# Pairs of tiles of one expert as seven block products for eight: a mixture-of-experts stage on one Trainium2 core

## The chip, the cores and the metric

The kernel runs on 1 core of one Trainium2 chip. The metric is the device time of one execution in microseconds (us). All runs below were in the fast state, but for one of the six of e1_static_after, and for single runs whose state is unknown; both are said where they come. Ratios are the mean time of one kernel's fast runs over the mean time of the other kernel's fast runs of the same rounds, on the same chip; so they are not quite the ratio of the medians that are quoted beside them.

Two sections of a run are used throughout, both read from the timeline of TensorE. The *stretch* goes from the first of the 48 small products with which the routing places its tokens (shortly before the tiles of the second round begin) to the end of the last product. The *tail* goes from there to the end of the span. What lies before the stretch, mostly attention, is the same code in every kernel here, yet it ended anywhere from 226 to 236 us after the start, in both kernels and in every experiment. That alone moves single times by 8 us or so; stretch and tail are free of most of it. The granted clock has a part in it: before the stretch, the profile of before (stretch from 234.71 us) has 0.50 for 10.24 us from 102.7 and for 3.41 us from 212.0, and that of after (226.49) has 1.00 from 9.2 us on.

## The reference

```python
def reference(q, k, v, w_gate, w_local, w1, w2):      # shortened
    x = attention(q, k, v)                            # (8, 576, 512), half local heads, half strided
    logits = x @ w_gate                               # 8 experts
    for b, s in every token in order:
        fresh = argmax(logits[b, s])
        e = fresh if s == 0 or sigmoid(x[b, s] @ w_local) < 0.5 else prev_e
        prev_e = e
        h = np.maximum(x[b, s] @ w1[e], 0.0)          # w1[e]: 512 x 1024
        out[b, s] = softmax(logits[b, s])[e] * (h @ w2[e])   # w2[e]: 1024 x 512
```

All is fp32. Which expert a token has depends on the data, so the kernel sorts the 4608 tokens on the chip into tiles of 128 tokens of one expert. For these inputs there are 6 early tiles (routed while attention still runs), then 30 whole tiles and 2 mixed ones (two half tiles of two experts).

## The kernel before

One tile is 32 hidden products into two PSUM banks, 4 transposes of the next tile, 8 output products, and one scatter by GpSimd. VectorE copies the transposed tile and works out the gates of its tokens, no more.

```python
    def hidden(self, j):
        nc = self.nc
        w1, xT, hT = self.w1t[j], self.xT[j], self.hT[j]
        for g in range(FK // self.HB):
            ps = self.bank()
            for i in range(self.HB):
                c = slice((g * self.HB + i) * P, (g * self.HB + i + 1) * P)
                for kk in range(DK):
                    ins = nc.tensor.matmul(ps[:, i], lhsT=w1[:, kk, c], rhs=xT[:, kk * P:(kk + 1) * P],
                                           start=(kk == 0), stop=(kk == DK - 1))
            nc.scalar.activation(hT[:, g * self.HB:(g + 1) * self.HB], ps, Act.Relu)
        return ins.ins

    def output(self, j):                              # cut: the branch for mixed tiles
            for kk in range(FK):
                ins = nc.tensor.matmul(ps, lhsT=self.hT[j][:, kk], rhs=self.w2t[j][:, kk, :],
                                       start=(kk == 0), stop=(kk == FK - 1))
        nc.scalar.activation(y, ps, Act.Copy, scale=self.pt[j])
        nc.gpsimd.indirect_dma_start(out=self.out, in_=y, ...)

    def run(self, ctx, second, check):                # cut to the loop
        for j, t in enumerate(self.T):
            ahead = self.weights(j + 2) if j + 2 < NT else []
            ...                                       # gathers, three tiles ahead
            if t["rd"] is self.r2 and NT_MIN - NE <= t["i"] < self.r2.whole:
                ...                                   # used: the number of whole tiles, read from SBUF
                ctx.enter_context(tc.If(used > t["i"]))
            ins = (self.hidden_mixed if "halves" in t else self.hidden)(j)
            ...                                       # first half of the weight loads
            if j + 1 < NT:
                self.turn_x(j + 1)
            ins = self.output(j)
            ...                                       # second half of the weight loads
```

Tiles that may or may not exist stand under nested conditions, so one jump at the end skips those that do not.

Of the kernel before, what the change touches and what calls it, by code (L numbers as in the profile page):

```python
# [18 lines left out]
P = 128  # L19
# [33 lines left out]
NT = NT_MAX + NM  # L53

MIXED = (14, 25)
SKIP = 8192
# [4 lines left out]
AHEAD = 3  # L61

# [39 lines left out]
class Round:  # L102
# [3 lines left out]
    def __init__(self, pool, whole, nm=0):  # L106
        self.whole, self.n = whole, whole + nm
        self.gi = pool.tile([P, self.n], I32, name="gi")
        self.si = pool.tile([P, self.n], I32, name="si")
        self.oh = pool.tile([P, self.n, E], F32, name="oh")  # L110
        self.et = pool.tile([1, self.n + 1 + 2 * nm], I32, name="et")
# [74 lines left out]
def passes(tc, careful, q, k, vl, vs, wg, w1, w2, out, xd, c, sums, bad):  # L186
    with ExitStack() as ctx:
        keep = ctx.enter_context(tc.tile_pool(name="keep", bufs=1))
        r1 = ctx.enter_context(tc.tile_pool(name="slots1", bufs=1))
        r1 = Round(r1, NE)  # L190
        r2 = ctx.enter_context(tc.tile_pool(name="slots2", bufs=1))
        r2 = Round(r2, NT_MAX - NE, NM)
# [18 lines left out]
        with ExitStack() as part:  # L211
            psr = part.enter_context(tc.tile_pool(name="psr", bufs=2, space=PSUM))
            rp = part.enter_context(tc.tile_pool(name="rp2", bufs=1))
            ex.run(part, route(tc, rp, psr, B, c, codes, r2, early),
                   None if careful else lambda: bounds(tc, rp, psr, sums, bad))
# [284 lines left out]
def route(tc, rp, pp, nb, c, codes, rd, early):  # L500
# [4 lines left out]
    R, CN, n, whole = nb * E, LT * nb, rd.n, rd.whole  # L505
# [61 lines left out]
    nc.tensor.matmul(ps[0:R, 0:1], lhsT=c.less[0:E, 0:R], rhs=nt[0:E], start=True, stop=True)  # L567
    first = nn[:, 3:4]
    if final:
        nc.vector.tensor_copy(first, ps[0:R, 0:1])  # L570
        tiles, skipped = nt, nn[:, 2:3]
    else:
        nc.vector.tensor_scalar(first, ps[0:R, 0:1], float(NE), None, Alu.min)
        tiles, skipped = nn[:, 2:3], None
        nc.vector.tensor_scalar(tiles, first, -1.0, float(NE), Alu.mult, Alu.add)
        nc.vector.tensor_tensor(tiles, tiles, nt, op=Alu.min)
        nc.vector.tensor_copy(early, tiles[0:E])
    end = rp.tile([E, 1], F32, name="end")
    nc.vector.tensor_tensor(end, first[0:E], tiles[0:E], op=Alu.add)
    over = rp.tile([E, whole], F32, name="over")  # L580
    nc.vector.tensor_scalar(over, c.io[0:E, 0:whole], end, None, Alu.is_ge)
    thr, base = nn[:, 4:5], nn[:, 5:6]
    nc.vector.tensor_scalar(thr, nn[:, 2:3], float(P), nn[:, 1:2], Alu.mult, Alu.subtract)
    if final:
        nc.vector.tensor_tensor(base, first, skipped, op=Alu.subtract)
        nc.vector.tensor_scalar(base, base, float(P), nn[:, 1:2], Alu.mult, Alu.add)
    else:
        nc.vector.tensor_scalar(base, first, float(P), nn[:, 1:2], Alu.mult, Alu.add)
# [4 lines left out]
    if final:  # L593

        last, far = nn[:, 9:10], nn[:, 10:11]
        nc.vector.scalar_tensor_tensor(last, nt, float(P), thr, Alu.mult, Alu.add)
        nc.vector.tensor_tensor(far, first, nt, op=Alu.add)
        nc.vector.tensor_scalar(far, far, -float(P), float(P * whole), Alu.mult, Alu.add)
        nc.vector.scalar_tensor_tensor(far, rank, float(HT), far, Alu.mult, Alu.add)
        more = rp.tile([R, S], F32, name="more")  # L600
        nc.vector.tensor_scalar(more, cum, last, far, Alu.is_gt, Alu.mult)
        nc.vector.tensor_tensor(slot, slot, more, op=Alu.add)
# [5 lines left out]
    nc.tensor.matmul(ps[:, 0:whole], lhsT=c.ones, rhs=over, start=True, stop=True)  # L608
    if final:
        nc.tensor.matmul(ps[0:1, n:n + 1], lhsT=c.ones[:, 0:1], rhs=nt[0:E], start=True, stop=True)  # L610
        nc.tensor.matmul(ps[0:1, n + 1:n + 1 + NH], lhsT=c.er[0:E], rhs=whose, start=True, stop=True)
        for h in range(2):
            nc.tensor.matmul(ps[:, whole:n], lhsT=c.half[h], rhs=whose.rearrange("e (m h) -> e h m", h=2)[:, h],
                             start=(h == 0), stop=(h == 1))
# [4 lines left out]
    nc.vector.tensor_scalar(rd.et[:, 0:n], ps[0:1, 0:n], float(E - 1), None, Alu.min)  # L619
    if final:  # L620
        nc.vector.tensor_copy(rd.et[:, n:], ps[0:1, n:n + 1 + NH])
    nc.vector.tensor_tensor(rd.oh, across(c.io[:, 0:E], [P, n, E]), spread(ps[:, 0:n], [P, n, E]), op=Alu.is_equal)
# [43 lines left out]
class Ring:  # L666


    def __init__(self, pool, n, shape, name):
        self.tiles = [pool.tile(shape, F32, name=f"{name}{i}") for i in range(n)]  # L670

    def __getitem__(self, j):
        return self.tiles[j % len(self.tiles)]


class Experts:

# [4 lines left out]
    def __init__(self, ctx, tc, xd, w1, w2, out, c, r1, r2):  # L682
        self.tc, self.nc = tc, tc.nc
        self.xd, self.w1, self.w2, self.out, self.c = xd, w1, w2, out, c
        self.r2 = r2
        xp = ctx.enter_context(tc.tile_pool(name="xp", bufs=1))
        self.w1t = Ring(xp, 2, [P, DK, F], "w1t")
        self.w2t = Ring(xp, 2, [P, FK, D], "w2t")
# [4 lines left out]
        self.pe = Ring(xp, 2, [P, E], "pe")  # L693
        self.pt = Ring(xp, 2, [P, 1], "pt")
        self.T = [dict(rd=r1, i=i, rows=BE * S) for i in range(NE)] + [dict(rd=r2, i=i, rows=N) for i in range(r2.whole)]
        for m, j in enumerate(MIXED):
            self.T.insert(j, dict(rd=r2, i=r2.whole + m, rows=N, halves=[r2.n + 1 + 2 * m + h for h in range(2)]))
        self.used = 0

    def weights(self, j, h=0):  # L700

        nc, t = self.nc, self.T[j]
        w1 = lambda e: self.w1[bass.ds(e, 1)].rearrange("o (k p) f -> p (o k) f", p=P)
        w2 = lambda e: self.w2[bass.ds(e, 1)].rearrange("o (k p) f -> p (o k) f", p=P)

        at = t["halves"][h] if "halves" in t else t["i"]

        def load(dst, src, part):
            if ("e", h) not in t:
                t["e", h] = nc.values_load(t["rd"].et[0:1, at:at + 1], engines=[ET.SP], min_val=0, max_val=E - 1,  # L710
# [3 lines left out]
            nc.sync.dma_start(out=dst[:, s], in_=src(t["e", h])[:, s])  # L714

        to = ((self.w1x, w1), (self.w2x, w2)) if h else ((self.w1t[j], w1), (self.w2t[j], w2))
        return [lambda a=a, part=part: load(*a, part) for a in to for part in range(2)]

    def gather(self, j):
        t = self.T[j]  # L720
        self.nc.gpsimd.indirect_dma_start(  # L721
            out=self.xg[j], out_offset=None, in_=self.xd[0:t["rows"]],
            in_offset=bass.IndirectOffsetOnAxis(ap=t["rd"].gi[:, t["i"]:t["i"] + 1], axis=0))

    def turn_x(self, j):
        nc, t = self.nc, self.T[j]
        x, ps = self.xg[j], self.psx[j]
        for kk in range(DK):
            nc.tensor.transpose(ps[:, kk * P:(kk + 1) * P], x[:, kk * P:(kk + 1) * P], self.c.ident)  # L729
        ins = nc.vector.tensor_copy(self.xT[j], ps)  # L730

        with self.tc.issue_after(ins.ins):
            nc.vector.tensor_tensor(self.pe[j], x[:, D:DX], t["rd"].oh[:, t["i"]], op=Alu.mult)
            nc.vector.tensor_reduce(self.pt[j], self.pe[j], axis=AX.X, op=Alu.add)

    def bank(self):
        self.used += 1
        return self.psh[self.used - 1]

    def hidden_mixed(self, j):  # L740

        nc, xT = self.nc, self.xT[j]
        for f in range(2):
            ps = self.bank().rearrange("p a b -> p (a b)")
            for kk in range(DK):
                for h, w1 in enumerate((self.w1t[j], self.w1x)):
# [5 lines left out]
    def turn_h(self, j, f):  # L752
        nc, ps = self.nc, self.bank()
        for i in range(self.HB):
            k = f * self.HB + i
            ins = nc.tensor.transpose(ps[:, i], self.h[:, k * P:(k + 1) * P], self.c.ident)
# [129 lines left out]
```

## Time and profile before

| | before |
|---|---|
| time, median of 3 runs | 746.26 us (744.17 to 748.84) |
| profiled run: span, stretch, tail | 750.2, 496.05, 19.44 us |
| TensorE, VectorE, ScalarE busy | 96%, 25%, 20% |
| weights and other hardware-queue traffic | 216.87 MB, 81.7% of 16 DMA engines |
| one tile, start to start | 14.45 us |

The stretch is 66% of the span and it is TensorE alone: the prediction below shows the lines and how they are read. Two more lines are needed later, the gathers and scatters of GpSimd (instructions, busy us, mean ns of one, and idle time before them):

```profile
L721 POOL DMA_INDIRECT xg<-xd,gi x41 | 40.3, 983 | 381.2 <-issue 139.0
L788 POOL DMA_INDIRECT out_dram<-y,si x38 | 40.8, 1075 | 266.5 <-ACT y L787 253.0
```

and the end of it, the last scatter of the timeline (start, length, and what it waited for), which starts 1.0 us after the last product ended at 730.7 us:

```profile
731.77 0.98 POOL L788 DMA_INDIRECT out_dram<-y,si  x1 [13.45 <-ACTq L211]
```

### The profile page before, as it was taken

How to read it: one execution, taken by the hardware profiler on the slowest of the kernel's cores; microseconds unless marked ns; L12 is line 12 of the kernel's file. 1: busy time of each engine (PE TensorE's matmuls, PEld its weight loads, DVE VectorE, ACT ScalarE, POOL GpSimd, SP SyncE). 2: the span in 40 equal slices, each digit the busy share in tenths (PEclk: the TensorE clock that was granted, in tenths of full speed). 3: DMA queues.
4: the chain of work that ended last, by engine and by line, in shares of the span. 5: the costliest groups of instructions: out<-in, count | busy, mean ns of one | idle time of the engine just before them, and what ended most of it. 6: DMA issues, size and time to landing. Idle time of an engine off the chain costs nothing. (4 is left out here: it accounts for less than half of the span.)

```text
span 750.2 us, 12762 instructions
## 1 busy us (share of the span) xinstructions
PE 722.9 (96%) x5132; PEld 546.1 (73%) x5132; DVE 183.8 (25%) x614; ACT 148.3 (20%) x267; POOL 84.4 (11%) x100
## 2 busy tenths in 40 slices
PE   7999999999999999999999999999999999999990
PEld 6999898977777667767736776776657677677660
DVE  5777877755360000000010000000010000000000
ACT  2555434541111111111111111111111111111110
POOL 1000002001012111111111111111111111111100
PEclk9999979999999999999999999999999999999995
DMA  9988778986868999999998989999997998999993
GB/s 345 346 275 272 266 216 306 337 305 213 305 236 287 328 335 324 348 403 395 376 352 287 324 310 345 372 401 398 368 319 284 345 330 307 334 335 314 323 321 118
DMA packets 95655, 238.24 MB, mean 318 GB/s; under 512 B 10526, under 2 KB 19742, under 8 KB 95584
## 3 DMA queue, kind: packets, MB, share of 16 engines
q1 hardware_dynamic: 88736, 216.87, 81.7%
q0 software_dynamic: 6320, 20.36, 7.0%
q8 instruction: 44, 0.72, 0.4%
q14 instruction: 27, 0.22, 0.1%
q10 hardware_dynamic: 528, 0.07, 0.1%
HBM read 218.26 MB, written 19.55 MB: 317 GB/s over the span
## 5 line engine op out<-in xcount | busy, mean ns | idle before, releaser
L768 PEld LDWEIGHTS hps<-xgT,w1t 128*128 128x128 f32 x2304 | 262.4, 192 | 16.0 <-issue 15.5
L768 PE MATMUL hps<-xgT,w1t 128*128 128x128 f32 x2304 | 263.8, 275 | 0.3 <-DVE xgT L730 0.3
L785 PE MATMUL yps<-w2t,hT 128*128 128x512 f32 x576 | 254.9, 596 | 0.0
L785 PEld LDWEIGHTS yps<-w2t,hT 128*128 128x128 f32 x576 | 107.2, 191 | 121.6 <-issue 121.6
L730 DVE COPY xgT<-tps 128x512 f32<-128x512 f32 x39 | 27.0, 691 | 424.8 <-PE tps L729 424.7
L770 ACT ACTIVATE hT<-hps 128x512 f32<-128x512 f32 x72 | 43.0, 597 | 216.3 <-PE hps L768 208.7
L721 POOL DMA_INDIRECT xg<-xd,gi x41 | 40.3, 983 | 381.2 <-issue 139.0
L787 ACT ACTIVATE y<-yps,pt 128x512 f32<-128x512 f32 x38 | 26.1, 687 | 261.2 <-PE yps L785 245.4
L788 POOL DMA_INDIRECT out_dram<-y,si x38 | 40.8, 1075 | 266.5 <-ACT y L787 253.0
L333 PE MATMUL sps<-qt,kt 64*128 64x96 f32 (+2 forms) x704 | 50.6, 290 | 5.3 <-DMA kt<-in_k_dram 5.0
L333 PEld LDWEIGHTS sps<-qt,kt 64*128 64x128 f32 (+2 forms) x704 | 44.5, 197 | 10.0 <-issue 8.2
L337 ACT ACTIVATE e<-sps 128x576 f32<-128x576 f32 (+1 forms) x64 | 39.9, 651 | 19.3 <-PE sps L333 18.2
L380 PE MATMUL vps<-vlt,e 128*96 128x96 f32 x384 | 40.8, 264 | 0.2 <-PE sps L333 0.2
L380 PEld LDWEIGHTS vps<-vlt,e 128*96 128x96 f32 x384 | 37.3, 176 | 4.1 <-issue 3.1
L380 PE MATMUL vps<-vst,e 108*108 108x108 f32 (+1 forms) x320 | 38.2, 275 | 1.0 <-DVE xs L391 0.8
L380 PEld LDWEIGHTS vps<-vst,e 108*108 108x108 f32 (+1 forms) x320 | 34.8, 185 | 2.7 <-PE vps L380 0.9
L340 DVE TENSOR_TENSOR e<-e,maskL 128x576 f32<-128x576 f32 x32 | 23.2, 754 | 17.9 <-ACT e L337 17.7
L340 DVE TENSOR_TENSOR e<-e,maskS 108x648 f32<-108x648 f32 (+1 forms) x32 | 23.1, 753 | 9.5 <-ACT e L337 9.5
L423 ACT COPY xT<-xps 128x324 f32<-128x324 f32 (+1 forms) x32 | 18.7, 684 | 33.0 <-PE xps L417 31.9
L729 PE MATMUL tps<-ident,xg 128*128 128x128 f32 x156 | 23.8, 274 | 0.0
L729 PEld LDWEIGHTS tps<-ident,xg 128*128 128x128 f32 x156 | 18.3, 142 | 0.2
L391 DVE TENSOR_TENSOR xl<-vps,rc 96x384 f32<-96x384 f32 x32 | 17.3, 545 | 0.5
(177 smaller groups left out, 318.8 us busy)
## 6 DMA issues: line engine op xcount, KB each, us to landing
w1t<-in_w_dram SPq DMA_DIRECT2D x80, 1024.0 KB
w2t<-in_w_dram SPq DMA_DIRECT2D x80, 1024.0 KB
kt<-in_k_dram SPq DMA_DIRECT2D x15, 608.0 KB
qt<-in_q_dram SPq DMA_DIRECT2D x15, 576.0 KB
vlt<-in_vl_dram SPq DMA_DIRECT2D x8, 780.0 KB
vst<-in_vs_dram SPq DMA_DIRECT2D x8, 650.0 KB
xd<-xl SPq DMA_DIRECT2D x8, 576.0 KB
w1x<-in_w_dram SPq DMA_DIRECT2D x4, 1024.0 KB
```

The costliest lines, as they stand in the source:

```text
L333: st["pe"] = nc.tensor.matmul(ps[0:kb, h, i * w:(i + 1) * w], lhsT=kt[r, u.i2, c:c + kb], rhs=qt[r, u.i2, c:c + w], start=True, stop=True)
L337: nc.scalar.activation(ev, ps[0:kb, :, 0:m * w], Act.Exp, bias=0.0, scale=1.0 / DH ** 0.5)
L340: nc.vector.tensor_tensor(blocks(ev, m), blocks(ev, m), mask, op=Alu.mult)
L380: nc.tensor.matmul(ps[0:w, o:o + w], lhsT=u.e[0:kb, h, i * w:(i + 1) * w], rhs=vt[0:kb, u.i2, u.t0 + i, c:c + w], start=True, stop=True)
L721: self.nc.gpsimd.indirect_dma_start(out=self.xg[j], out_offset=None, in_=self.xd[0:t["rows"]], in_offset=bass.IndirectOffsetOnAxis(ap=t["r ...
L729: nc.tensor.transpose(ps[:, kk * P:(kk + 1) * P], x[:, kk * P:(kk + 1) * P], self.c.ident)
L730: ins = nc.vector.tensor_copy(self.xT[j], ps)
L768: ins = nc.tensor.matmul(ps[:, i], lhsT=w1[:, kk, c], rhs=xT[:, kk * P:(kk + 1) * P], start=(kk == 0), stop=(kk == DK - 1))
L770: nc.scalar.activation(hT[:, g * self.HB:(g + 1) * self.HB], ps, Act.Relu)
L785: ins = nc.tensor.matmul(ps, lhsT=self.hT[j][:, kk], rhs=self.w2t[j][:, kk, :], start=(kk == 0), stop=(kk == FK - 1))
L787: nc.scalar.activation(y, ps, Act.Copy, scale=self.pt[j])
L788: nc.gpsimd.indirect_dma_start(out=self.out, in_=y, in_offset=None, bounds_check=N - 1, oob_is_err=False, out_offset=bass.IndirectOffsetOn ...
```

## The change

Two whole tiles of one expert become a pair. Its 256 tokens by 512 inputs, and the weights, are each cut into 2 x 2 blocks, and each layer is done as seven block products for eight (Strassen's form in Winograd's arrangement). The block sums of the weights, of x and of h go to VectorE; four of the seven products of a layer are added up in one PSUM bank, and ScalarE copies the bank out between them. An odd tile of an expert stays single. The pairs 0 to 8 and the two mixed tiles, which always exist, come first; then eight places for singles under nested conditions; then places for seven more pairs under nested conditions. With these inputs 4 singles and 4 of those pairs exist: 13 pairs in all.

```diff
+    def sums_b(self, t, blocks):
+        v, (b11, b12, b21, b22) = self.nc.vector, blocks
+        v.tensor_tensor(t[:, 0], b12, b11, op=Alu.subtract)
+        v.tensor_tensor(b12, b22, b12, op=Alu.subtract)
+        v.tensor_tensor(t[:, 1], b22, t[:, 0], op=Alu.subtract)
+        v.tensor_tensor(t[:, 2], b21, t[:, 1], op=Alu.subtract)
...
+    def hidden_pair(self, j):                       # cut: names of the blocks, product and row
+        self.sums_b(self.t2, self.blocks_w(w2))
+        product(chain, a11, b11, True)
+        nc.scalar.copy(out=p, in_=chain)
+        product(b7, s3, t3, True)
+        product(chain, s2, t2, False)
+        nc.scalar.copy(out=u, in_=chain)
+        product(b2, a12, b21, True)
+        row(b2, p, flat[0])
+        nc.vector.tensor_tensor(u, b7, u, op=Alu.add)
+        product(chain, s1, t1, False)
+        nc.scalar.copy(out=v, in_=chain)
+        row(b7, v, flat[3])
+        product(b4, a22, t4, True)
+        row(b4, u, flat[2])
+        product(chain, s4, b22, False)
+        nc.scalar.activation(flat[1], chain, Act.Relu)
+        self.sums_a(self.hs, hs)
...
+    def output_pair(self, j):                       # the same form, 256 columns, and two scatters
...
+        singles, pairs = count(1, E), count(0, PAIR_MAX)
+        with ExitStack() as chain:
+            for j in range(first, last):
+                chain.enter_context(tc.If(singles > j - first))
+                run(j)
+        for j in range(last, len(U)):
+            ctx.enter_context(tc.If(pairs > U[j]["pair"]))
+            run(j)
```

Here `product` is one block product (8 calls of matmul in the hidden layer, 4 in the output layer), and `row` adds a bank to a saved part on VectorE and applies the ReLU on ScalarE. In the order of a unit, the x sums and the first-layer weight sums of the next unit follow the hidden products of this one, before its output products. The rest of the diff (new slots in the routing, PSUM banks as one ring of eight, buffers) is cut.

## The prediction

> **What bounds the kernel now.** I read the page's busy shares and slices first, then the groups, then the instructions in order of time late in the run, then what TensorE waited for.
>
> ```profile
> PE 722.9 (96%) x5132; PEld 546.1 (73%) x5132; DVE 183.8 (25%) x614; ACT 148.3 (20%) x267; POOL 84.4 (11%) x100
> ...
> DVE  5777877755360000000010000000010000000000
> ...
> DMA  9988778986868999999998989999997998999993
> ...
> L768 PE MATMUL hps<-xgT,w1t 128*128 128x128 f32 x2304 | 263.8, 275 | 0.3 <-DVE xgT L730 0.3
> ...
> L785 PE MATMUL yps<-w2t,hT 128*128 128x512 f32 x576 | 254.9, 596 | 0.0
> ```
>
> TensorE is busy 96% of the span; DVE is all but idle after slice 12, which is where the expert stage begins; the DMA engines are nearly full there. Busy TensorE is not yet a bound, since weights that just arrive would look alike. The idle columns decide: 0.3 us before all 2304 hidden products and 0.0 before all 576 output products. Nothing makes TensorE wait, so only less work on it helps. The timeline gives the unit cost:
>
> ```profile
> 687.25 7.31 PE L768 MATMUL hps<-xgT,w1t 128*128 128x128 f32 x64
> 694.40 0.60 PE L729 MATMUL tps<-ident,xg 128*128 128x128 f32 x4
> 694.83 7.03 PE L785 MATMUL yps<-w2t,hT 128*128 128x512 f32 x16
> 701.70 7.31 PE L768 MATMUL hps<-xgT,w1t 128*128 128x128 f32 x64
> ```
>
> From start to start: 7.15 us for 64 hidden instructions (111.7 ns each), 0.43 us for 4 transposes, 6.87 us for 16 output instructions (429.3 ns each); 14.45 us a tile. The source has 32 hidden and 8 output products per tile, so an fp32 product is two instructions. The groups' means (275 and 596 ns) [...] are not what one costs; the spacing is.
>
> **How many pairs.** Counting the tokens per expert from the inputs gives 6 early tiles, then 30 whole and 2 mixed ones, which the trace confirms (72 evictions of hT, two per whole tile; 38 of y). Per expert the 30 are 4, 3, 4, 3, 3, 4, 4, 5: 13 pairs and 4 singles. Not all 36 whole tiles gain, only 26.
>
> [...] At N=256, which this kernel lacks in this stage, [...] the line through the two measured spacings gives 217.6, which I use. [...]
>
> ```profile
> L340 DVE TENSOR_TENSOR e<-e,maskL 128x576 f32<-128x576 f32 x32 | 23.2, 754 | 17.9 <-ACT e L337 17.7
> ```
>
> [...] The trace has two long ones on TensorE's sequencer:
>
> ```profile
> L211 PEldq COMPARE_BRANCH  x6: 65/76/6040, 667.0 to 731.0; - x6
> ...
> L130 PEldq COMPARE_BRANCH  x1: 6806/6806/6806, 731.6 to 731.6; - x1
> ```
>
> The skipped tiles cost 6.04 us of branch, but from about 724.2, some 6.5 us before the last product ended: the sequencer runs ahead, and it is hidden. [...]
>
> **The change, part by part.**
> Hidden products of a pair: seven block products of 8 calls, 56 calls or 112 instructions, at the same 128 columns: 112 x 111.7 = 12.51 us, where two tiles take 14.30. Saved 1.79.
> Output products: seven of 4 calls, 28 calls or 56 instructions, at 256 columns: 56 x 217.6 = 12.19 us against 13.74. Saved 1.55; the fixed cost per instruction eats some of the eighth, since 56 short instructions replace 32 long ones.
> Transposes: 8, 0.86 us, unchanged. A pair is thus 25.56 us for 28.90, 3.34 less, and 13 pairs save 43.4 us.
>
> Added on DVE[...]: eight block sums of the two weights over 1024 elements, 8 x 1.22 = 9.8; four sums each of h (512) and x (256), 2.8 + 1.7; four PSUM additions of 512 and four of 256, about 2.7 + 1.6; gates 0.3. That is 18.9 us in 25.6, 74%: it fits, with DVE's total rising to about 400 us. ACT: about 7.9 us a pair, 31%. Both lie beside the products as long as order allows.
>
> Order matters, so I laid one steady pair out from the built order of instructions, time zero at its first hidden product (1.79 us each). DVE runs the next pair's first weight sum (after the fifth product frees its buffer, 9.0 to 10.2), the row for h22, the in-place weight sum, the row for h21 (11.9 to 12.5), another weight sum (to 13.6), then three sums of h; the one that the third output product needs is ready at about 15.6. That product starts at 12.51 + 0.86 + 2 x 1.74 = 16.85. Margin 1.2 us: no stall in steady state. The interleaved bank gives every chain copy (0.69 us) a whole product to hide behind.
>
> Moved: weights are fetched once per pair. About 31 sets of 4 MB instead of 42, so the DMA share should fall from nine tenths to about seven. That saves no time now, as TensorE never waited for DMA; it protects the result.
>
> What I charge:
> First pair: its gathers begin one tile earlier than needed; one follows a scatter (0.7 us ACT, 1 us POOL, 1 us its own issue, 6.5 us to landing, about 9) where the transposes ask at 7.6. About 1 us.
> Mixed tiles: their hT copies stand behind weight sums in DVE's queue, about 1.2 us each, 2.4 in all.
> Leaving the singles: these are nested conditions with code behind them now. TensorE drains, loads the pair count, branches; in the old kernel's tail that took 0.9 us (load at 731.2, branch at 731.6, last product over at 730.7). I charge 1.1. But the SP's way out waits for all its DMA lanes, and unneeded prefetches (two singles that do not exist) land about 8.3 us after the last product, as the old tail shows. So the second dynamic pair's w1 is asked for at about +9.5 us and lands at +14 and +17; DVE's sum of it stands ahead of rows that the current pair needs; the h sum comes at about 21.8 instead of 18.0. Charge 3.8.
> Route: 42 columns for 35 in one string of 48 small products, 0.3. Short waits, 0.2 a pair, 2.6. A second scatter at the end, 0.5.
> Sum of charges 1 + 2.4 + 1.1 + 3.8 + 0.3 + 2.6 + 0.5 = 11.7. So 746.3 - 43.4 + 11.7 = 714.6; I say 714 us.
>
> **Rivals.**
> First, DVE becomes the bound. At 74% it has no room for a wrong order; if each DVE row costs 0.2 us more [...] (some 32 rows a pair) the margin of 1.2 is gone and each pair waits 2 or 3 us: 13 x 2.5 = 33, about 745 us, no gain. Against it: [...] back to back they overlap a little (the 0.69 us copy at 709.49 is followed by the next DVE instruction at 710.09). For it: TensorE now has waits on DVE and ACT inside every pair where it had none[...].
> Second, the branch structure costs more: [...] 6 us that the sequencer cannot hide, because semaphores inside a pair hold it back, at the pair conditions or leaving the singles. One such 6 us gives 720; five, on every dynamic pair, 740. Against: fall-through branches are 65 to 76 ns, and only the exits jump.
> Third, weights were the hidden bound and fewer bytes help too. Against: 0.0 us of waiting; then nothing comes beyond the 43.4, and the best case is about 703 us.
> Fourth, the 256-column products are slower than the line says, say 235 ns: 56 x 17 ns is 1 us a pair, 13 us, 727.
>
> **Range and chances.** The product arithmetic is firm: it rests on spacings that repeat to the hundredth, so 703 is a floor. The charges are soft, mostly upward. Range 707 to 724. Two per cent faster is below 731.3: it would take charges of 28 us, more than twice mine, so 0.94 faster, 0.05 same, 0.01 slower.
>
> **What would show it.** Right: pair products spaced 111.7 and about 217 ns; a steady pair 25.6 us from start to start; TensorE idle before its products under 15 us in all, most of it once, in the first pair after the singles, with DVE or a w1 load as what ended it; TensorE busy about 680 us; DVE about 400; DMA near seven tenths; the tail after the last product still about 19 us (730.7 to 750.2). Wrong: idle before the third output product in every pair means that the DVE margin was mis-sized; a pair of 27 us or more without idle means the 256-column spacing was; a gap with nothing running on any engine at the singles' exit means the branch.

## The result, and the profile after

| | before | after |
|---|---|---|
| time, median of 4 runs each, same rounds | 745.21 us (743.17 to 748.84) | 719.61 us (716.16 to 724.57) |
| ratio of the fast runs, 95% interval | | 0.9656 [0.9586, 0.9726] |
| profiled run: span | 750.2 us | 714.5 us |
| stretch, tail | 496.05, 19.44 us | 464.24, 23.77 us |
| start of the stretch | 234.71 us | 226.49 us |

The profiled runs differ by 35.7 us, but 8.2 of that lies before the stretch, in code that did not change: the profile of before had one of the slow attention stages and that of after a quick one. The change itself is worth 31.8 us in the stretch and costs 4.3 in the tail, 27.5 in all, in keeping with the 25.6 between the medians.

The page of the changed kernel, parts 1, 2 and 3 (busy time; tenths in 40 slices; one DMA queue):

```profile
PE 673.8 (94%) x5244; PEld 577.7 (81%) x5244; DVE 399.6 (56%) x894; ACT 192.0 (27%) x360; POOL 100.7 (14%) x103
...
PE   7999999999999999999999999999999979999960
...
DVE  6777888755273348656366664558610026676630
...
DMA  9988779985878996785867857786678989755660
...
q1 hardware_dynamic: 71136, 170.73, 67.9%
```

TensorE has 49 us less to do, VectorE 216 us more, and the traffic fell by 46 MB: all three are close to what was foreseen (TensorE about 680 us busy, VectorE about 400, the traffic down from nine tenths). TensorE's row is full but for the first slice, the 33rd, and the end. VectorE's row shows where the singles are, by two zeros. A steady pair in the timeline, from the start of its first product to the start of the next pair's (start, length, and the number of instructions last):

```profile
285.66 1.95 PE L839 MATMUL bank<-xT,w1t 128*128 128x128 f32 x16
287.44 1.95 PE L839 MATMUL bank<-xs,w1t 128*128 128x128 f32 x16
...
298.16 1.04 PE L839 MATMUL bank<-ident,xg 128*128 128x128 f32 x8
299.03 1.89 PE L839 MATMUL bank<-w2t,h 128*128 128x256 f32 x8
300.76 1.89 PE L839 MATMUL bank<-t,h 128*128 128x256 f32 x8
302.49 1.89 PE L839 MATMUL bank<-t,hs 128*128 128x256 f32 x8
...
311.12 1.95 PE L839 MATMUL bank<-xT,w1t 128*128 128x128 f32 x16
```

The reader is to take starts, not lengths: 1.79 us a hidden product (16 instructions, 111.7 ns each), 0.87 for the transposes, 1.727 an output product (8 instructions, 215.9 ns each, for the 217.6 that were interpolated), and 25.46 us for the pair. Nothing waits in it. The tightest place is the sum of h that the third output product needs; of another pair, the sum on VectorE and the product:

```profile
393.49 0.68 DVE L813 TENSOR_TENSOR hs<-hs,h 128x512 f32<-128x512 f32 x1
...
395.20 1.03 PE L839 MATMUL bank<-t,hs 128*128 128x256 f32 x4
```

The sum is done at 394.17, 1.03 us before the product starts (1.2 had been worked out from the order of the built instructions); the count of 4 is only where the view was cut off. The waits of TensorE in the stretch, from the list of waits (total us, times, longest):

```profile
PE bank L839 <- issue: 5.2, 1, 5.2
...
PE bank L839 <- DMA xg<-xd,gi: 1.7, 2, 1.2
PE bank L839 <- DVE hs L813: 1.3, 2, 0.9
...
PE bank L970 <- DVE hT L944: 0.3, 1, 0.3
```

One entry of 5.2 us, once, with nothing named as its cause, stands out. It lies where the singles end and the next pair begins. The timeline there, cut to four instructions:

```profile
573.62 7.03 PE L974 MATMUL bank<-w2t,hT 128*128 128x512 f32 x16
585.83 3.55 PE L839 MATMUL bank<-xT,w1x 128*128 128x128 f32 x16 [5.17 <-issue]
589.17 2.09 PE L839 MATMUL bank<-xs,w1x 128*128 128x128 f32 x16
591.01 0.18 DVE L805 TENSOR_TENSOR pe<-xg,oh 128x16 f32<-128x16 f32 x1 [11.68 <-DMA xg<-xd,gi]
```

and the branches of the conditions on TensorE's sequencer in that window (shortest, median and longest in ns; the two starts):

```profile
L1074 PEldq COMPARE_BRANCH  x2: 4256/5235/6214, 574.1 to 580.8; - x2
```

The last product of the last single ends about 580.6. The first branch, 6.2 us from 574.1, runs while the products still go: it is hidden, as before the change (6.04 us from 724.2, with the last product over at 730.7). The second begins at 580.8, when TensorE is empty, and takes 4.3 us in the open. Then the first product of the pair takes 3.34 us from start to start instead of 1.79 and the second 1.93: the record of the granted clock has 1.00 in the gap and until 586.05, 0.2 us after the first product began, and 0.50 for 3.41 us from there. VectorE, meanwhile, has stood 11.7 us before the gate of the pair after, whose gathers GpSimd issued only when it had left the singles; its sums come late, and the third output product of this pair waits 0.93 us more.

What the whole passage costs can be read from the transposes: the ones of a single that does not exist begin at 573.19, those of the second pair after the singles at 600.03, those of the third at 626.67 (the first pair's were done before the singles). Without a loss the steps would be 0.43 + 6.87 + 12.51 = 19.81 us and 25.47; they are 26.84 and 26.64. The loss is 7.0 + 1.2 = 8.2 us. The expectations quoted below say 8.6, because they measure against the run without conditions and count the 0.43 us of those useless transposes too.

At the end, two scatters where there was one:

```profile
688.64 1.02 POOL L980 DMA_INDIRECT out_dram<-y,si  x1 [17.61 <-DVE y L907]
693.51 1.01 POOL L980 DMA_INDIRECT out_dram<-y,si  x1 [3.85 <-DVEq L132]
```

and GpSimd's way out of the pair conditions (semaphore waits, the longest 5546 ns; then INC_SWDGE_SEM, which took 1.81 us and is called the closing of GpSimd's DMA queue here):

```profile
L218 POOLq EVENT_SEMAPHORE  x4: 17/43/5546, 693.7 to 699.5; - x4
...
L218 POOLq INC_SWDGE_SEM  x1: 1814/1814/1814, 699.6 to 699.6; - x1
```

The first scatter landed at 692.67; the second began at 693.51, 4.9 us after the first. (The wait is put down to a DVE sequencer instruction here; in e9, where the same two scatters stand earlier, it is put down to the landing of the first, 3.88 us.) GpSimd's long semaphore wait, at the end of the conditions, runs from 693.79 to 699.34; the second scatter landed at 699.30. Before the change it closed the same queue at 731.8, straight after the one scatter at 731.77, which landed at 740.83. The tail is 23.77 us, of which the prediction knew 19.9.

### The profile page after: what moved, and what is told of

The parts are those of the page before. It is cut to its first block, busy times and chain, and to the rows that moved or that the text cites. A ratio compares the mean times of both kernels' runs of the same rounds, so it can differ in the third digit from the quotient of the medians.

```text
span 714.5 us, 13302 instructions
## 1 busy us (share of the span) xinstructions
PE 673.8 (94%) x5244; PEld 577.7 (81%) x5244; DVE 399.6 (56%) x894; ACT 192.0 (27%) x360; POOL 100.7 (14%) x103
## 5 line engine op out<-in xcount | busy, mean ns | idle before, releaser
L783 POOL DMA_INDIRECT xg<-xd,gi x44 | 48.0, 1091 | 250.9 <-DVE rc L394 112.9
L956 PEld LDWEIGHTS bank<-xgT,w1t 128*128 128x128 f32 x640 | 72.6, 192 | 3.1 <-issue 1.9
L956 PE MATMUL bank<-xgT,w1t 128*128 128x128 f32 x640 | 73.6, 276 | 0.9 <-DVE xgT L801 0.9
L974 PE MATMUL bank<-w2t,hT 128*128 128x512 f32 x160 | 70.3, 592 | 0.0
L839 PE MATMUL bank<-xs,t 128*128 128x128 f32 x416 | 50.7, 275 | 0.0
L839 PE MATMUL bank<-t,hs 128*128 128x256 f32 x208 | 49.4, 380 | 1.3 <-DVE hs L813 1.3
L839 PEld LDWEIGHTS bank<-xs,t 128*128 128x128 f32 x416 | 48.5, 192 | 0.0
L839 PEld LDWEIGHTS bank<-xT,w1t 128*128 128x128 f32 x384 | 45.7, 192 | 2.6 <-issue 2.1
L839 PE MATMUL bank<-xT,w1t 128*128 128x128 f32 x384 | 47.4, 276 | 0.0
L839 PE MATMUL bank<-xs,w1t 128*128 128x128 f32 x384 | 46.8, 275 | 0.0
L839 PE MATMUL bank<-w2t,h 128*128 128x256 f32 x192 | 45.4, 379 | 0.0
```

What stands on the lines that cost most here:

```text
L783: self.nc.gpsimd.indirect_dma_start(out=u["xg"][:, a] if "pair" in u else u["xg"], out_offset=None, in_=self.xd[0:u["rows"]], in_offset=ba ...
L839: self.end = fn(*args, **kw).ins
L956: ins = nc.tensor.matmul(ps[:, i * P:(i + 1) * P], lhsT=w1[:, kk, c], rhs=xT[:, kk * P:(kk + 1) * P], start=(kk == 0), stop=(kk == DK - 1))
L974: ins = nc.tensor.matmul(ps, lhsT=hT[:, kk], rhs=w2[:, kk, :], start=(kk == 0), stop=(kk == FK - 1))
```

## The experiments

The theory after reading the two traces: (a) the pair arithmetic is right, and VectorE has a margin of 1 us that nothing steady uses up; (b) what was lost is lost at the conditions, 8 us where the singles end and 4 in the tail. The rivals: VectorE is the bound and paces the pairs; or the short waits in every pair, or the first pair, hold the loss; and for the way out, that it is the branch alone, the gathers alone, or the weights. Losses at the way out are computed as in the section above, from transposes to transposes, for each kernel against its own products and the period of its own pairs after the singles. The table collects what follows, all from the profiled runs:

| run | time, median us | ratio to before | stretch | tail | steady pair | loss at the way out |
|---|---|---|---|---|---|---|
| before | 743.8 to 747.4 | 1 | 496.05 | 19.44 | 28.90 (two tiles) | |
| after | 719.61 | 0.9656 | 464.24 | 23.77 | 25.47 | 8.2 |
| r0_after | 724.68 | 0.9687 | 466.69 | 23.92 | 25.47 | 8.8 |
| e1_static_after | 704.66 | 0.9427 | 454.78 | 14.93 | 25.47 | 0 |
| e2_static_before | 743.54 | 0.9973 | 495.61 | 13.48 | | |
| e3_five_slots | 721.52 | 0.9678 | 464.54 | 23.71 | 25.47 | 8.5 |
| e4_eight | 761.72 | 1.0203 | 501.45 | 24.74 | 28.98 | 1.5 |
| e5_output_seven | 742.12 | 0.9908 | 480.43 | 24.36 | 27.25 | 1.3 |
| e6_hidden_seven | 755.71 | 1.0083 | 494.01 | 24.33 | 27.85 | 10.5 |
| e7_dve_one | 732.36 | one run | 470.40 | 24.12 | 25.60 | 7.9 |
| e8_dve_four | 753.36 | one run | 492.22 | 24.14 | 25.95; 28.41 and more under conditions | 11.5 |
| e9_pairs_first | 710.46 | 0.9530 | 459.32 | 19.45 | 25.47 | 3.3 |
| e10_five_early | 713.47 | 0.9569 | 457.49 | 23.83 | 25.47 | 1.3 |
| e11_eight_early | 720.89 | 0.9690 | 465.04 | 24.51 | 25.47 | 8.5 |

All of them gave the right result. The 95% intervals of the ratios are 0.004 to 0.007 to each side; they are given where they matter.

### r0_after: the changed kernel again, in five rounds

No edit.

> The changed kernel once more, to have its ratio with more rounds and a second profile. Expected ratio 0.965 within 0.006. If the traces' difference is the whole story, the stretch from the start of the 48 route products to the last product is 464 us again (496 in the kernel before) and the tail after the last product 24 us (19.5 before). The attention stage differs by some 8 us between the two profiles at hand although its code is the same: that should vary from run to run in both kernels.

Measured: 724.68 us median (717.32 to 726.00, 6 runs), ratio 0.9687 [0.9633, 0.9740]. The 5.5 us gap at the same place is there again, so it belongs to the kernel and not to one run. The stretch is 2.4 us longer than in the first profile, and most of that is the first pair: TensorE waited 1.95 us for a gather (0.53 and 1.18 in two parts in the first profile), and the 16 output products that followed took 8.57 us from start to start for 6.87, a loss of 1.70 us. By the author's estimate that is a lower clock: 3.41 us at a granted 0.50, as the first profile has them after its gap, would cost as much.

### e1_static_after and e2_static_before: no conditions at all

Both kernels with the counts of these inputs written in, which gives the right result for these inputs only.

```diff
 # e1_static_after: E singles -> 4, PAIR_MAX pairs -> 13, and
-        with ExitStack() as chain:
-            for j in range(first, last):
-                chain.enter_context(tc.If(singles > j - first))
-                run(j)
-        for j in range(last, len(U)):
-            ctx.enter_context(tc.If(pairs > U[j]["pair"]))
-            run(j)
+        for j in range(first, len(U)):
+            run(j)
 # e2_static_before: r2.whole tiles -> 30, and
-                ctx.enter_context(tc.If(used > t["i"]))
```

> The changed kernel with the counts of this data written in (4 singles, 13 pairs) and no conditions. Main theory (leaving the singles costs 5.2 us of branch, about 1.7 us of cold TensorE clock and 1 us of late DVE sums, and the conditions lengthen the tail): the stretch falls by about 8 us to 456, the tail from 24 to 19 or less, in all 10 to 14 us under the changed kernel, about 707 us. Rival (the conditions are hidden, and the pairs themselves are what is slower than worked out): within 3 us of the changed kernel.

> The kernel before with its 30 tiles written in and no conditions on tiles. Main theory: its conditions are hidden (TensorE never waits), so the stretch stays 496 us and only the tail can shorten, by 0 to 3 us: same within 0.5%. If it gains as much as the static pair kernel does, conditions cost both kernels alike and are no reason for the shortfall.

Measured: 704.66 us (698.36 to 708.29, the 5 fast runs; a sixth of 709.67 counts as slow and is left out), ratio 0.9427 [0.9368, 0.9486], and 743.54 us (736.89 to 746.29, 6 runs), ratio 0.9973 [0.9922, 1.0023]. Without conditions the changed kernel is 20 us quicker, 9.5 to 11.9 of it in the stretch and 8.9 in the tail. The kernel before has the same stretch as with conditions (495.61 against 496.05); only its tail is 6.0 us shorter. So conditions cost the old kernel nothing while it computes, and the new one some 10 us. This is (b). The tails were a miss: that of the kernel before fell by 6.0 where 0 to 3 was said, and the 20 us of the changed kernel are more than the 10 to 14 expected, mostly by its tail. The traces show one thing that is gone: GpSimd closes its queue (1.4 to 1.8 us) once, at the end, where it did so twice in the kernel before and three times in the changed one; at the end, and after the pairs, it first waits for what is in flight (in the kernel before the last scatter landed at 740.83 and the queue was closed at 741.03; in the changed one, after the pairs, 699.30 and 699.55).

### e3_five_slots: five places for singles instead of eight

```diff
-        self.U += [dict(rd=r2, at=PAIR_MAX + i, ..., single=i) for i in range(E)]
+        self.U += [dict(rd=r2, at=PAIR_MAX + i, ..., single=i) for i in range(5)]
```

With five places one single is skipped instead of four, and one is loaded in vain instead of two. Right for these inputs only.

> The changed kernel with five places for singles instead of eight (right for this data, which has four): leaving them skips one tile's code instead of four. If the exposed branch is the jump out of the skip block over the code of the others, the gap before the first pair after the singles falls from 5.2 us to under 2 us; and as the SP then skips no weight loads it need not wait for its queues, so the later wait of 1 us on DVE goes too: 4 to 7 us faster than the changed kernel. [...]

Measured: 721.52 us (717.17 to 724.93, 6 runs), ratio 0.9678 [0.9630, 0.9726]: no gain, the expectation failed, and how it failed was the best lead of the study. TensorE's waits in its own list, and VectorE in the timeline:

```profile
PE bank L839 <- ACT part L876: 4.4, 1, 4.4
...
PE bank L839 <- ACTq L1074: 1.1, 1, 1.1
```

```profile
593.99 0.18 DVE L805 TENSOR_TENSOR pe<-xg,oh 128x16 f32<-128x16 f32 x1 [14.10 <-DMA xg<-xd,gi]
```

The branches were short (176 and 235 ns) and the gap at the singles' end only 1.1 us. But now TensorE stood 4.4 us in the middle of the pair, for a copy of the chain bank. Behind that copy is VectorE: it stands 14.1 us before the gate of the next pair, first in its queue, because its gathers come only after GpSimd has left the singles; the additions of the running pair stand behind it. The 8.5 us are thus 1.1 at the exit, 4.4 behind VectorE, 2.6 at the lower clock that came with that second wait (granted 0.50 from 596.19 for 6.83 us), and 0.4 of small change. In the changed kernel this wait (11.7 us) had been there too, hidden behind the 5.2 us gap. One cause had covered another of about the same size.

### e4_eight, e5_output_seven, e6_hidden_seven: the form taken back, whole or by layer

Pairs stay as they are, with their order, buffers and conditions, but both layers (e4), the hidden layer (e5) or the output layer (e6) are done as eight block products, without the block sums that are then not needed.

```diff
 # e4, both layers; e5, this layer only
-        product(chain, a11, b11, True)
-        ...                                    # seven products, parts, rows
+        for r in range(2):
+            for c in range(2):
+                ps = self.bank()
+                ...                            # two block products added in the bank
+                nc.scalar.activation(flat[2 * r + c], ps, Act.Relu)
 # e4 and e6, the output layer: the same, with scale=U["pt"][:, r:r + 1]
```

> The changed kernel with the same pairs, order, weights once per pair and conditions, but eight block products for eight in both layers and no block sums. Main theory (only the count of products pays): a pair takes 14.30 hidden + 0.87 transposes + 64 x 0.216 = 13.82 output, 28.99 us from start to start instead of 25.47, so 13 x 3.5 = 46 us more than the changed kernel, about 765 us, and 2 to 3% slower than the kernel before although it fetches a quarter fewer bytes. Rival (sharing the weights pays): at or under the time of the kernel before, 745 us or less.

> Seven products in the output layer only, eight in the hidden layer. Main theory: a pair takes 14.30 + 0.87 + 12.09 = 27.26 us, 13 x 1.79 = 23 us more than the changed kernel, about 743 us. If one layer's sums on DVE were what holds the pair, taking one layer's away would give back part of this and it would be nearer to 735.

> Seven products in the hidden layer only, eight in the output layer. Main theory: 12.51 + 0.87 + 13.82 = 27.20 us a pair, 13 x 1.73 = 22 us more than the changed kernel, about 742 us; this and the output-only kernel should add up to the eight-product kernel. The rival of DVE as the bound: nearer to 735.

Measured: e4 761.72 us (759.03 to 764.53, 4 runs), ratio 1.0203 [1.0157, 1.0248]; e5 742.12 us, 0.9908 [0.9851, 0.9966]; e6 755.71 us, 1.0083 [1.0021, 1.0146]. The pair arithmetic shows cleanly in the steady pairs: 25.47 with both layers in seven, 27.25 with the output layer alone (1.79 more, one hidden product), 28.98 with neither. So the form is worth 28.98 - 25.47 = 3.51 us a pair, 45.6 over 13.

The stretches, though, grew by only 37.2 and 16.2 us where 46 and 23 were expected, and by 29.8 where 22 was. Both shortfalls are of about one size and have one place: the way out costs 1.5 and 1.3 us in e4 and e5, for 8.2. In both the branch was short, and in both the hidden layer has no additions on VectorE, so a VectorE that stands before a late gate holds up nothing. e6 keeps the additions of the hidden layer, and there the loss is the full 10.5 us, the largest single piece of it the longest of these waits:

```profile
PE bank L839 <- ACT h L864: 7.5, 10, 4.0
```

(4.0 once, behind VectorE, at the way out; and about 0.39 in most other pairs, since without the block sums in between the output layer asks for the last rows of h at once: part of e6's excess.) That e5 and e6 would add up to e4 did not come true: 16.2 and 29.8 us against 37.2. What the study gains: without the form, the pairs alone are a loss of 2% against the kernel before, mostly by the tail (5.3 us) and the stretch (5.4).

### e7_dve_one and e8_dve_four: how much room VectorE has

One, and four, sums of h more than needed in each pair, ahead of the sums that the third output product waits for. The result stays right.

```diff
+        for _ in range(n):                     # n = 1, or 4
+            nc.vector.tensor_tensor(self.hs[:, 0], hs[2], hs[3], op=Alu.add)
         self.sums_a(self.hs, hs)
```

> One extra sum of h (about 0.65 us on VectorE) ahead of the sums that the third output product waits for, in each of the 13 pairs; the result stays right. Theory: in a steady pair the sum is ready 1.03 us before its product (394.17 against 395.20 us in the changed kernel's trace), so the period stays at 25.47 us and only the pairs that already waited (0.36 and 0.93 us) wait 0.6 us longer: the expert stretch grows by 1 to 2 us over the 464.2 to 466.7 us of the changed kernel. Rival, VectorE is the bound and its rows set the pace: 0.6 x 13 = 8 us longer, a period of 26.1 us.

> The changed kernel with one block sum of h (512 elements, 0.69 us) done five times, four of them for nothing, ahead of the sum that the third output product waits for. The profile of the changed kernel shows that sum ready at 394.17 where the product starts at 395.20, 1.0 us of margin; here it comes about 3.2 us later. Main theory: the third output product of each pair waits 2.2 us, a pair takes 27.7 us, the stretch from the route products to the last product grows by about 28 us. If DVE had several microseconds of slack, nothing; if it were the bound already, 13 x 3 = 40 us.

Measured, one run each, state unknown: 732.36 and 753.36 us; both also had a slow attention stage, so the stretches are what counts. One row: 470.40 us, 3.7 to 6.2 over the changed kernel, between the theory's 1 to 2 and the rival's 8. The steady pair went from 25.47 to 25.60, so the row is nearly hidden there, as the margin says; what grew is a wait of 1.3 and 1.5 us in the two pairs before the mixed tiles. The margin is not the same in every pair, and the theory had taken it as one.

Four rows: 492.22 us, 28.0 over the first profile of the changed kernel. In the pairs that stand under conditions the wait before the third output product is

```profile
660.08 1.97 PE L839 MATMUL bank<-t,hs 128*128 128x256 f32 x8 [2.71 <-DVE hs L813]
```

and with the margin of 1.03 that makes 3.74 us by which the sum came later: four rows of 0.60 us from start to start, and four sums of x (0.34 each) that slipped in between. In the pairs without conditions the scheduler hid it: the built order had moved 22 instructions of the next pair's hidden products (16 make one) ahead of the third output product, and those pairs took 25.95. So the total of e8 is not 13 equal waits: 3 to 5 us of it falls on each of the last three pairs, on the pair before the singles and on one before a mixed tile, and some 3 more than in the changed kernel on the way out. That the sum of 28 us was the one foreseen is luck. Together the two runs say that VectorE is no bound in the kernel as it is, and that it becomes one where its sums come more than a microsecond later.

### e10_five_early and e11_eight_early: the gathers of the second pair asked for before the singles

```diff
             at = max(ahead - 2, last if j > last else NE - 1)
+            if j == last + 1:
+                at = first - 1
             gathers.setdefault(at, []).append(j)
```

e10 has this on top of e3's five places, e11 on the changed kernel with its eight. The buffer that the gathers fill is free there.

> Five places for singles, as in the run with five slots, and the gathers of the second pair after the singles moved ahead of the singles (its buffer is free there). In the run with five slots TensorE stood only 1.1 us where the singles end, but lost 8.9 us all the same over the next two pairs, 4.4 us of it behind VectorE, whose queue stood 14.1 us before a gate that needs these gathers. Theory: the gathers, late by the way out of the singles and first in VectorE's queue, are what kept the loss: it falls to 1 to 3 us, the stretch to 456 to 459 us, the time to 713 to 716 us where the five slots gave 721.5. Rival: the weights of that pair are as late and VectorE's sums of them stand in the same place: the loss stays at 6 us or more and the time within 2 us of 721.

> The changed kernel with its eight places and only the gathers of the second pair after the singles moved ahead of the singles: the fourth corner of places (eight or five) and gathers (late or early). The losses at the way out so far: 8.6 us (eight, late), 8.9 (five, late), about 1 (five, early). Theory: with eight places two unneeded singles are being loaded when TensorE leaves, and SP asks for the next pair's first weights only when they have landed, 8 to 9 us after; VectorE then waits for those weights instead of the gathers, and TensorE's own late branch of some 4 us stays too: the loss is 5 to 9 us, the stretch 461 to 465 us, the time 717 to 721 us. Rival: the gathers alone are the cause, whatever the number of places: the loss falls to 1 to 3 us, as with five, or to 5 at most if the long branch comes back, and the time to 713 to 716 us.

Measured: e10 713.47 us (711.94 to 715.74, 4 runs), ratio 0.9569 [0.9524, 0.9614]; e11 720.89 us (720.77 to 724.86, 4 runs), ratio 0.9690 [0.9630, 0.9750]. The losses at the way out make a square:

| | gathers late | gathers early |
|---|---|---|
| eight places (long branch) | 8.2 and 8.8 us | 8.5 us |
| five places (short branch) | 8.5 us | 1.3 us |

Neither half helps the time alone; both together take away the loss. With the gathers early and the branch long, the gap and the slow products after it cost all 8.5 us by themselves, and VectorE keeps up: the wait of 0.93 us for its sum is gone. In this one profile the slow products hide that gain, for they cost 2.9 us here (3.54 and 2.93 us from start to start, for 1.79) and 1.7 and 1.9 in the two profiles of the changed kernel. The three products:

```profile
589.86 3.75 PE L839 MATMUL bank<-xT,w1x 128*128 128x128 f32 x16 [5.44 <-issue]
593.40 3.09 PE L839 MATMUL bank<-xs,w1x 128*128 128x128 f32 x16
596.33 1.95 PE L839 MATMUL bank<-xs,t 128*128 128x128 f32 x16
```

With both, the first product of the pair waits 1.1 us for the counts and takes 1.86 us from start to start:

```profile
585.47 2.02 PE L839 MATMUL bank<-xT,w1x 128*128 128x128 f32 x16 [1.08 <-ACTq L1076]
587.33 1.95 PE L839 MATMUL bank<-xs,w1x 128*128 128x128 f32 x16
```

e11 also refutes a part of its own theory: SP asked for the next pair's weights at 593.43, as late as foreseen, but VectorE did not wait for them; at 601.89 it waited for a bank of TensorE. The late weights had no effect in that run; eight places with a short branch and early gathers, where they might, were not run.

What stays open is why the second branch is long. It took 4.3 to 4.7 us in three builds with eight places (the changed kernel in both its profiles, e7, e11) and 0.2 us in four others with eight places (e4, e5, e6, e8), so it is not the number of places as such. e7 and e8 differ only by three more repeats of one sum on VectorE, and e7 has the long branch and e8 not. The program of each engine differs in length and in waits from build to build; no run here shows which of these makes the branch long.

### e9_pairs_first: the pairs that may not exist before the singles

```diff
-        self.U += [dict(rd=r2, at=PAIR_MAX + i, ..., single=i) for i in range(E)]
-        self.last = len(self.U)
         self.U += [pair(k) for k in range(PAIR_MIN, PAIR_MAX)]
+        self.last = len(self.U)
+        self.U += [dict(rd=r2, at=PAIR_MAX + i, ..., single=i) for i in range(E)]
...
-                chain.enter_context(tc.If(singles > j - first))
+                chain.enter_context(tc.If(pairs > U[j]["pair"]))
...
-            ctx.enter_context(tc.If(pairs > U[j]["pair"]))
+            ctx.enter_context(tc.If(singles > j - last))
```

with the early gather of e10 for the second single. All places stay, so it serves any routing, as the changed kernel does.

> The same work for any routing, with the places whose number depends on the data in the other order: first the pairs, then the eight places for singles, so that what follows the first way out has no block sums on VectorE and what ends the kernel is one scatter at a time; the gather of the second single is asked for before. Theory: the loss at the way out (8.6 us in the changed kernel) falls to the branches themselves plus a short wait for the weights, 2 to 6 us, and the tail of 23.8 us falls to 19 to 20 us, that of the kernel before: together 6 to 11 us, a time of 709 to 715 us, with the conditions all still there. Rival: any way out of a set of conditions costs this much, whatever stands behind it: the time stays at 720 within 3 us.

Measured: 710.46 us (707.69 to 711.80, 4 runs), ratio 0.9530 [0.9490, 0.9569], as the theory said. It beats both kernels; its interval lies below both of the changed kernel's. Its stretch is 459.32 and its tail 19.45 us. At the way out, after the last pair, the first product of a single waits 3.0 us,

```profile
628.51 7.38 PE L956 MATMUL bank<-xgT,w1x 128*128 128x128 f32 x64 [3.03 <-issue]
```

and the loss there is 3.3 us (transposes to transposes 23.37, without loss 0.87 + 12.09 + 7.15 = 20.11). Nothing on VectorE holds a single back. And the kernel ends with one scatter at a time:

```profile
687.55 0.99 POOL L980 DMA_INDIRECT out_dram<-y,si  x1 [12.16 <-ACTq L218]
```

1.0 us after the last product at 686.55, with GpSimd's queue closed at 688.0, as in the kernel before. The second scatter of the last pair and GpSimd's wait for it still take place, but at 628 to 637 us, beside the singles. So the 4.3 us of the tail came from what stands last, not from the conditions being there.

## Why the prediction was right or wrong

The call (faster, at 714, with 707 to 724) was right; the time was 719.61 us, 5.6 over the number. Term by term, from the profiled runs:

| term, as the prediction put it | predicted us | measured us |
|---|---|---|
| pairs, 13 of them | -43.4 | -44.7 (13 x (28.90 - 25.465)); by e4, -45.6 |
| first pair's gathers | 1 | 1.7; 1.95 + 1.70 of slow products in the repeat |
| mixed tiles | 2.4 | 0.34 in the first, and 0.36 in the pair before the second |
| leaving the singles: drain and branch 1.1, late sums 3.8 | 4.9 | 8.2: gap 5.2, slow clock 1.7, late sum 0.93, rest 0.4 |
| short waits, 0.2 a pair | 2.6 | none outside the rows above |
| transposes of a pair that is not there | not seen | 0.86 |
| route | 0.3 | not told apart |
| second scatter at the end | 0.5 | 4.3 |

*The bound and the pair.* Right. TensorE's products set the time, and the spacing of the two sizes gave the pair to 0.1 us (25.56 predicted, 25.47 measured). The 256-column spacing was off by 1.7 ns, in the kernel's favour; that rival is gone, and so is the one in which fewer bytes help: with 46 MB less there is nothing beyond the pair arithmetic.

*VectorE.* Right, and closer than one should like. The times of its rows were the author's estimate; the trace of after has 1.22 us for a sum of 1024 elements, 0.69 at 512 and 0.42 at 256, and 0.69 and 0.48 for the additions of 512 and 256, with the gates 19.2 us a pair for the 18.9 of the prediction. And a margin of 1.03 us for 1.2, shown to be real by e7 (the steady pair hides the extra row but for 0.13 us) and to be all there is by e8.

*Leaving the singles.* The place was right and the size wrong, by 3.3 us, and the step that failed is the sentence "in the old kernel's tail that took 0.9 us ... I charge 1.1". The prediction saw the long branch, and took it as hidden, since the old trace showed it begun before the last product ended. There were two branches to pass, and the second begins only when TensorE is empty: 0.2 us in the old tail, 4.3 here. The prediction quotes a case of 6.8 us in the open (the branch at 731.6, after the last product at 730.7) and charges nothing like it. It is the prediction's second rival, in its mild form ("one such 6 us gives 720"). The second half of the term, sums that come late because of SP's way out, had the right shape (the weights were asked for 10.5 us after the last product, where +9.5 was foreseen) but another cause ranked first: the gathers, which are late because of GpSimd's way out and which the prediction did not follow beyond the first pair. e3 with e10 shows that the gathers, not the weights, hold VectorE when the branch is short; and in e11 the weights cost nothing, behind a long branch. By the prediction's own signs, the gap should have been ended by VectorE or a load of w1; it was ended by nothing that the profile names, which is near the sign it gave for the branch.

The lower clock after the gap was not charged at all: after 5.17 us of idle the trace has a granted clock of 0.50 for 3.41 us, and 3.34 us for a product of 1.79.

*The tail.* "A second scatter at the end, 0.5" is the term that missed most for its size. It counted the issue of a second scatter and not that it waits for the first to land, and that GpSimd's way out of the pair conditions waits for it in turn. Why it waits there is not shown: at the exit of the singles, and in the kernel before, it closes its queue straight after the scatter is issued. The sign that the tail would stay at 19 us failed. e9, where the same work stands before the singles, has the tail of the kernel before.

*The small charges.* The mixed tiles and the short waits were charged 5.0 us and cost 0.7. They were put in as caution, and they paid for the misses: the stretch fell by 31.8 us where the terms said 32.2, which looks exact and is not. The terms that were measured add up to -44.7 + 1.7 + 0.7 + 8.2 + 0.9 = -33.2 us; 1.4 us of the stretch is not told apart. "703 is a floor" held for the medians: even without conditions the same pairs took 704.66 us. Single runs of that kernel go down to 698, but the kernel before varies by 9 us in the same rounds.

*The working.* Its sums are right but for two of its rivals: 13 x 2.5 us on top of 714 gives 747, not 745, and five branches of 6 us give 744, not 740. Nothing rests on them.

## What to carry to other kernels

When work under conditions ends and other work follows, follow every engine out of it, not only the one that sets the time: what each of them asks for only after it has left (gathers, loads), and what stands behind that in the same engine's queue (in e3 VectorE stood 14.1 us before one gate, and TensorE 4.4 us for additions behind it). A gap may hide a second one of the same size, so a fix that "does nothing" is a reason to look where the wait went (here it moved from TensorE's sequencer to VectorE's queue) and to try both fixes together. And put last what ends quickly: the same two scatters cost 4 us at the end of the kernel and nothing before the singles.

## What else these runs measured

- The time of a compare and branch. In the profiles of before and after, 12 of TensorE's 20 took 65 to 86 ns, two 192 and 196 ns, and six 4.3 to 6.8 us; all of ScalarE's took 34 to 55 ns. Over all runs, those of TensorE at the way out of a set of conditions took 176 to 235 ns, or 3.3 to 7.5 us, both within the same run in most.
- Which gaps had slow products after them. A gap of 1.95 us between transposes (r0_after) was followed by 16 instructions at 8.57 us for 6.87, and one of 2.83 us between products (e8) by a product of 3.65 us in length for some 1.95, and so was one of three gaps of 2.71 us in e8 (the next product took 2.71 us for 1.73), while the other two and one of 3.03 us (e9) were not. So no length that divides the two kinds shows here. Up to the end of the work, the stretches with a granted clock of 0.50 lasted 3.41 and 10.24 us in before, 3.41 in after and 6.83 in e3.
- The spacing of fp32 products. Each is two instructions here, and these were spaced 111.7, 215.9 and 429.3 ns at 128, 256 and 512 columns.
- The cost of scattering twice in a row: at the end of the changed kernel the second scatter starts 4.9 us after the first, 0.8 us after the first landed, and closing the queue takes GpSimd another 1.5 us at the exit of the singles and 1.8 at that of the pairs.
- GpSimd's instructions beside VectorE's sums. With the sums (after) the scatters took 1300 ns in the mean for 1075 before, and the gathers 1091 for 983; with pairs but no sums (e4) 1134 and 979. The medians of the scatters were 1016, 1015 and 1012 ns, so a few long ones, up to 5.8 us, make the means. What made those long is not shown.
